# Output rows stored from two issuing queues, and another order for the last attention layer, in an interleaved S4 and sliding-attention kernel

## The chip, the cores and the metric

The kernel runs on one core of one Trainium2 chip. The time is the device time of one execution in microseconds (us), from the first to the last work of the program; each kernel is run several times and the median is given. The core's engines are TensorE (PE in the profile; PEld is its weight load), VectorE (DVE), ScalarE (ACT), GpSimd (POOL) and SyncE (SP, which here only issues DMA transfers). Each engine works through its own instructions strictly in the order in which the program gives them to it.

## The reference, cut to what matters

Four layers on a residual of 2048 positions by 512 channels in bfloat16: a state-space convolution (S4) and a sliding, dilated attention, twice.

```python
def _B_ref(x, wqkv, wo):                 # H = 32 heads of 16, W = 8, dil = 2
    qkv = (x @ wqkv).reshape(B, S, 3, H, Dh).transpose(2, 0, 3, 1, 4)
    q, k, v = qkv[0], qkv[1], qkv[2]
    idx = pos[:, None] - (jnp.arange(W) * dil)[None, :]
    mask = idx >= 0
    kg, vg = k[:, :, idx_c, :], v[:, :, idx_c, :]      # clipped at position 0
    logits = jnp.einsum("bhsd,bhswd->bhsw", q, kg) * scale
    attn = _softmax(jnp.where(mask[None, None], logits, -1e9), axis=-1)
    o = jnp.einsum("bhsw,bhswd->bhsd", attn, vg)
    return o.transpose(0, 2, 1, 3).reshape(B, S, D) @ wo

x = A_u
x = x + _A_ref(_layernorm(x), A_re, A_im, B_re, B_im, C_re, C_im, log_dt, Dskip)
x = x + _B_ref(_layernorm(x), wqkv, wo)
x = x + _A_ref(_layernorm(x), A_re, A_im, B_re, B_im, C_re, C_im, log_dt, Dskip)
x = x + _B_ref(_layernorm(x), wqkv, wo)
return x
```

## The kernel before

The residual stays on the chip in one tile X: 128 positions on the partitions, and on the free axis two halves of 256 channels, each with 16 row blocks (j = 0 to 15). The layers run one after the other: the convolution's kernel with the first convolution, `b_layer`, `a_layer`, `b_layer`. Only the last `b_layer` is touched by the change.

**How an order is made.** A layer does not emit instructions as it is written. It records operations in a `Plan`: `pl.op(engine, us, fn, *after)` is one step with the steps it comes after; `pl.either(name, way, way, ...)` records several ways of doing the same step. `Plan.run` then goes through a list of numbers, one string of `ORDERS` for each layer, and calls the functions in that order. A way whose numbers are not in the string does not exist in the program. So the string decides both the order on every engine and which engine does a step. The times and lags given to `pl.op` have no effect in the kernel.

**What the last layer does.**
- `start(q)`, for each quarter q of the positions (four row blocks) and each half cp of the channels: the block of X is turned so that channels lie on the partitions, either by a DMA transpose that SP issues (L1307) or by TensorE into the tile `pt_x` (L1301) and a copy (L1304). VectorE makes the layer norm's statistics (L1359) and joins them (L1363), ScalarE makes the roots (L1374).
- `pair` and `proj`: TensorE's q and k projections into `ps_qk` (L1439, L1420; four matmuls of 512 columns a group, or eight for a pair) and the copies to qT and kT (L1444, L1425), on ScalarE or VectorE. The keys of earlier positions are put beside the others by ScalarE, VectorE or a DMA (L1462).
- `pairs`: the norm's factors of neighbouring rows, moved down one partition by a small matmul (L1401), multiplied, spread by ScalarE to the tile RR (L1386), with POOL's ones for the first rows (L1392).
- `values`: v into VX (L1474, L1485, L1498).
- logits: VectorE's products of q and shifted k (L1519), a matmul that sums over a head's 16 channels into Lp (L1530), a copy to LT (L1548), a transpose into `pt_l` (L1556), a copy to L (L1561), and the multiplication by RR (L1599).
- softmax on VectorE (the sum's first step is L1580), with ScalarE and POOL.
- products with the values (L1695), summed by TensorE into `po`: either the flat way, 512 columns at a time (L1711), with a copy to `ot` (L1729) and a transpose back by TensorE (L1741) or by DMA (L1734); or the way of 128 columns (L1716) whose result needs no turn, with one copy (L1731).
- `out`: the output projection `ps_o` (L1795) and the residual's addition into X, in one of three ways: a VectorE addition (L1767); a ScalarE copy (L1773) and a VectorE addition (L1776); or a ScalarE copy and a DMA from POOL's queue that adds into X (L1779).
- `stored`: for each row block j a DMA of 128 rows by 512 channels to the output, after its addition, issued by SP (L1941).

Tiles are shared by rings: the products L1519 and L1695 have four buffers, `ps_qk` and most `ps_o` share two, `pt_x`, `po` and others two more.

Of the kernel before, what the change touches and what calls it, by code (L numbers as in the profile page):

```python
# [19 lines left out]
S = 2048  # L20
# [135 lines left out]
def halves(a):  # L156
    return a.rearrange("p (h c) -> p h c", h=2)
# [6 lines left out]
def turned_view(U):  # L164
    return U[:].rearrange("p j c -> p (j c)").rearrange("c (h j t p) -> c h j t p", h=2, j=NJ, t=2)
# [65 lines left out]
def load_params(nc, pp, prm):  # L231
# [75 lines left out]
]  # L307


# [1551 lines left out]
def kernel(  # L1861
# [16 lines left out]
    nc = tc.nc  # L1878
# [11 lines left out]
    X = kernel_and_first_conv(nc, tc, C, prm, A_u[0], const, kt_dram, eps, Wt)  # L1890
# [8 lines left out]
    ov = out[0].rearrange("(p j) d -> p j d", j=NJ)  # L1899
    with tc.tile_pool(name="mid", bufs=1) as mid:  # L1900
        U = mid.tile([128, NJ, D], BF, name="U")

        def summed(j, ps):
            if j // 4 not in BN_Q:
                nc.scalar.activation(X[:, :, j, :], halves(ps), ACT.Identity, accum_out=ln.sum[:, j:j + 1])
            else:
                nc.scalar.copy(X[:, :, j, :], halves(ps))

        def normed(pl, q, after):
            j0, j1 = q * 4, q * 4 + 4  # L1910

            def square(j):
                nc.scalar.activation(halves(U[:, j, :]), X[:, :, j, :], ACT.Square, bias=ln.nm[:, j:j + 1],
                                     accum_out=ln.sq[:, j:j + 1])

            def norm(j):
                nc.scalar.activation(halves(U[:, j, :]), X[:, :, j, :], ACT.Identity, bias=ln.nb[:, j:j + 1],
                                     scale=ln.rstd[:, j:j + 1])
            if q in BN_Q:
                for k in (j0, j0 + 2):  # L1920
                    o = [pl.op("V", 0.6, lambda j=j: ln.gather(X, 0, j, j + 1), after[j - j0]) for j in (k, k + 1)]
                    o = [pl.op("V", 0.09, lambda j=j: ln.gathered(j, j + 1), o[j - k]) for j in (k, k + 1)]
                    o = pl.op("A", 0.2, lambda k=k: ln.root(k, k + 2), *o)
                    o = pl.op("V", 0.08, lambda k=k: ln.offset(k, k + 2), o)
                    for j in (k, k + 1):
                        pl.mark(("u", j), pl.either(("norm2", j), lambda: pl.op("V", 0.32, lambda j=j: ln.norm(halves(U[:, j, :]), X[:, :, j, :], j), o),
                                                    lambda: pl.op("A", 0.71, lambda j=j: norm(j), o)))
                return
            o = pl.op("V", 0.12, lambda: nc.vector.tensor_scalar(ln.nm[:, j0:j1], ln.sum[:, j0:j1], -1.0 / D, None, ALU.mult),
                      *after)  # L1930
            o = [pl.op("A", 0.62, lambda j=j: square(j), o) for j in range(j0, j1)]
            o = pl.op("A", 0.2, lambda: ln.root_of_squares(j0, j1), *o)
            o = pl.op("V", 0.09, lambda: ln.offset_by(j0, j1), o)
            for j in range(j0, j1):
                a = pl.either(("norm2", j), lambda: pl.op("A", 0.71, lambda j=j: norm(j), o),
                              lambda: pl.op("V", 0.32, lambda j=j: ln.norm(halves(U[:, j, :]), X[:, :, j, :], j), o))
                pl.mark(("u", j), a)

        def stored(pl, q, after):
            for j, a in enumerate(after, q * 4):  # L1940
                pl.op("S", 0.45, lambda j=j: nc.sync.dma_start(ov[:, j, :].rearrange("p (h c) -> p h c", h=2), X[:, :, j, :]), a, lag=2.2)  # L1941
        b_layer(nc, tc, C, X, Wt, VX, turned_view(U), pst, eps, ln, True, summed, normed, BN_Q)
        a_layer(nc, tc, C, X, kt_dram, U)
        b_layer(nc, tc, C, X, Wt, VX, turned_view(U), pst, eps, ln, False, lambda j, ps: nc.scalar.copy(X[:, :, j, :], halves(ps)), stored, range(4))


# [28 lines left out]
```

## Time and profile before

| | us |
|---|---|
| Median of 3 runs | 431.56 (431.14 to 432.34) |
| Profiled execution, its own time | 430.11 |
| Span in the profile | 428.3 |
| Mean granted clock of TensorE | 0.999 of full speed |
| Last layer begins (first statistics) | 313.0 |
| Last addition into X ends | 423.8 |

All views are of one execution. Its own time is 1.8 us over the span, and 1.45 us under the median of the runs. In a timeline a row is a run of like instructions: start, duration, engine, line, operation, output tile <- input tile with shapes, the count after x, and in brackets the idle time ahead of it with what ended it. A DMA is seen twice: in the queue of the engine that issues it (SPq, ACTq), and as a transfer; "to landing" is from issue to the end of the transfer.

### The profile page before, as it was taken

To read this page: it belongs to the slowest core of one execution; us is meant where nothing else is said; L and a number is where in the kernel's file an instruction comes from. 1 tells how busy PE (TensorE), PEld (TensorE's weight loads), DVE (VectorE), ACT (ScalarE), POOL (GpSimd) and SP (SyncE) were. 2 spreads that over 40 slices of the span, in tenths; PEclk is the share of its full clock that TensorE was granted. 3 is DMA by queue.
4 is the path that set the end of the run, shared out by engine and by line. 5 is a ranking of instruction groups with operands and counts; after the bars stand their busy time and mean duration, and the time that the engine had idled before them with its cause. 6 is when DMAs were issued, how large, how long until landed. Compare 5 with 4: busy or idle time off the path is not lost.

```text
span 428.3 us, 11576 instructions
## 1 busy us (share of the span) xinstructions
PE 370.3 (86%) x4797; PEld 233.4 (54%) x4834; DVE 402.2 (94%) x682; ACT 320.9 (75%) x524; POOL 27.7 (6%) x97
## 2 busy tenths in 40 slices
PE   1277868897998889999997899899999999998995
PEld 1153646776887664347643345678864346643452
DVE  6999999999999789999899999999999899999994
ACT  6999999999998664668752578999957678752431
POOL 1000000000000200000000600020000000000240
PEclk9999999999999999999999999999999999999999
DMA  8996257597987774011223595199960000324295
GB/s 221 210 299 235 93 83 156 136 174 173 180 130 141 145 173 103 0 38 54 76 56 63 139 223 132 36 181 198 193 100 12 37 2 2 87 85 87 40 158 160
DMA packets 102203, 51.49 MB, mean 120 GB/s; under 512 B 81851, under 2 KB 94028, under 8 KB 101894
## 3 DMA queue, kind: packets, MB, share of 16 engines
q1 hardware_dynamic: 98758, 45.24, 49.1%
q0 software_dynamic: 3104, 5.24, 6.1%
q8 instruction: 38, 0.62, 0.7%
q10 hardware_dynamic: 288, 0.26, 0.2%
q14 instruction: 15, 0.12, 0.1%
HBM read 19.30 MB, written 6.29 MB: 60 GB/s over the span
## 4 chain that ended last, share of the span: by engine, by line
PE 48%; DVE 15%; ACT 14%; issue 4%; DMA 1%; ACTq 0%; DVEq 0%
PE po L1711 8%; PE ps_v L1474 7%; PE ps_qk L1420 7%; PE ps_qk L1439 6%; DVE prod L1695 5%; PE ps_o L1795 4%; PE Lp L1530 4%; PE psk L483 3%; DVE prod L1519 3%; ACT Z L875 2%; DVE pa L967 2%; PE ps_s L1117 2%; PE ps_s L872 1%; ACT sp_k L903 1%; PE vp L1183 1%
## 5 line engine op out<-in xcount | busy, mean ns | idle before, releaser
L1695 DVE TENSOR_TENSOR prod<-VX,L 128x512 bf16<-128x512 bf16 (+2 forms) x72 | 75.4, 1099 | 1.8 <-ACT VX L1485 1.0
L1519 DVE TENSOR_TENSOR prod<-qT,kT 128x4096 bf16<-128x4096 bf16 (+1 forms) x40 | 72.1, 1859 | 2.2 <-ACT kT L1462 1.0
L1711 PE MATMUL po<-prod,sb_ident 128*128 128x512 bf16 x233 | 56.4, 379 | 2.8 <-DVE prod L1695 2.0
L1711 PEld LDWEIGHTS <-sb_ident 128*128 128x128 bf16 x240 | 23.1, 97 | 31.3 <-issue 4.1
L875 ACT CAST Z<-ps_s 128x1024 bf16<-128x1024 f32 (+1 forms) x36 | 32.0, 932 | 0.5 <-PE ps_s L872 0.4
L1474 PE MATMUL ps_v<-wv,U 128*128 128x256 bf16 x256 | 31.4, 273 | 0.6 <-ACT VX L1485 0.3
L1795 PE MATMUL ps_o<-wo_t,oT 128*128 128x512 bf16 x124 | 31.4, 379 | 0.3 <-ACT oT L1744 0.2
L1729 ACT CAST ot<-po 128x1024 bf16<-128x1024 f32 (+1 forms) x16 | 15.1, 958 | 21.2 <-PE po L1711 21.2
L1420 PE MATMUL ps_qk<-U,wqk 128*128 128x512 bf16 x128 | 30.7, 380 | 0.3 <-ACT L L1658 0.3
L1485 ACT ACTIVATE VX<-ps_v,rs 128x256 bf16<-128x256 f32 x64 | 26.7, 473 | 5.6 <-PE ps_v L1474 5.1
L1439 PE MATMUL ps_qk<-U,wqk 128*128 128x512 bf16 x128 | 29.3, 379 | 0.0
L1474 PEld LDWEIGHTS <-U 128*128 128x128 bf16 x256 | 24.3, 97 | 8.9 <-issue 3.1
L1530 PE MATMUL Lp<-prod,sb_bones 128*32 128x512 bf16 x256 | 22.9, 383 | 3.0 <-DVE prod L1519 2.9
L1359 DVE BATCH_NORM_STATS2 pst<-X 128x6 f32<-128x256 bf16 x64 | 21.8, 407 | 0.5 <-ACT X L1209 0.5
L1420 PEld LDWEIGHTS <-wqk 128*128 128x128 bf16 x128 | 11.8, 98 | 16.8 <-issue 3.6
L1439 PEld LDWEIGHTS <-wqk 128*128 128x128 bf16 x128 | 12.2, 98 | 15.4 <-issue 1.6
L1795 PEld LDWEIGHTS <-oT 128*128 128x128 bf16 x128 | 12.2, 98 | 14.7 <-ACT oT L1744 0.7
L872 PE MATMUL ps_s<-KT,FK 128*128 128x128 bf16 (+1 forms) x360 | 18.8, 209 | 1.6 <-ACT KT L845 0.7
L967 DVE TENSOR_TENSOR pa<-sp_u,sp_k 128x2048 bf16<-128x2048 bf16 x16 | 19.3, 1220 | 0.8 <-ACT sp_k L903 0.5
L1171 DVE TENSOR_TENSOR pa<-xc,Kt 128x2048 bf16<-128x2048 bf16 x16 | 18.9, 1218 | 0.6 <-PE vp L1183 0.3
L892 PE MATMUL xp<-zt,sb_C 128*128 128x512 bf16 x45 | 15.0, 380 | 5.0 <-ACT zt L912 2.3
L872 PEld LDWEIGHTS <-FK 128*128 128x128 bf16 x360 | 17.4, 98 | 3.2 <-issue 2.3
(230 smaller groups left out, 841.1 us busy)
## 6 DMA issues: line engine op xcount, KB each, us to landing
kt_scratch<-sp_k SPq DMA_DIRECT2D x16, 256.0 KB, 3.0
Kt<-kt_scratch POOLq DMA_DIRECT2D x16, 256.0 KB, 6.6
sp_u<-sp_u SPq DMA_DIRECT2D x18, 128.0 KB, 2.7
X<-in_A_u_dram SPq DMA_DIRECT2D x8, 256.0 KB, 5.4
X<-in_A_u_dram SPq DMA_DIRECT2D x4, 512.0 KB, 5.6
Kt<-kt_scratch SPq DMA_DIRECT2D x8, 256.0 KB, 4.2
out_dram<-X SPq DMA_DIRECT2D x16, 128.0 KB, 2.0
VX<-VX SPq DMA_DIRECT2D x4, 448.0 KB, 3.7
```

The lines of the kernel that those rows point to most:

```text
L872: nc.tensor.matmul(ps[:, r, 0:n // 4, jj * 4:(jj + 1) * 4], w, x, start=(k == 0), stop=(k == len(todo) - 1))
L875: nc.scalar.copy(box["Z", kind, dc, b0][:, 0:n // 4, :, jq * 16:(jq + 1) * 16].rearrange("p g r k -> p r g k"), box.pop(("s1", kind, dc, j ...
L967: nc.vector.tensor_tensor(pr[:], box["U"][:, s:t + 1:t - s], k[:].unsqueeze(1).to_broadcast([128, 2, 1024]), ALU.mult)
L1420: nc.tensor.matmul(ps[:], wqk[:, ct, f0:f0 + 128], XT[:, ct // 2, 4 * s:4 * s + 4, ct % 2, :], start=(ct == 0), stop=(ct == 3))
L1439: nc.tensor.matmul(box[name][:, k * 512:k * 512 + 512], wqk[:, ct, f0:f0 + 128], XT[:, ct // 2, 4 * s:4 * s + 4, ct % 2, :], start=(ct == ...
L1474: nc.tensor.matmul(ps[:, jj].rearrange("p t h d -> p (t h d)"), XT[:, ct // 2, j + jj, ct % 2, :], wv[:, ct, fp * 256:(fp + 1) * 256], sta ...
L1485: nc.scalar.activation(out, ps, ACT.Identity, scale=r)
L1519: nc.vector.tensor_tensor(pr[:], windows(q, 0, 2), windows(kT[fp][:, a:a + n2, col(w):col(w) + 1024], -DIL * 128, 2), ALU.mult)
L1530: nc.tensor.matmul(Lp[r0:r0 + 32, w // 4, :], bones[:, w % 4 + k, :], pr[:, k, f2 - a, hb * 512:(hb + 1) * 512], start=(n == 1 and k == 0) ...
L1695: nc.vector.tensor_tensor(p2[:].rearrange("p w j t d h -> p w (j t) d h"), windows(v, -DIL * 256, taps), l.to_broadcast([128, taps, nj * 2 ...
L1711: nc.tensor.matmul(po[:, c:c + 512], ident[:], p2[:, t, k + j:k + j + 2].rearrange("p j t d h -> p (j t d h)"), start=first, stop=stop)
L1795: nc.tensor.matmul(ps, oT[:, ft // 2, o:o + 128], wo_t[:, ft, :], start=(ft == 0 and not res), stop=(ft == 3))
```

## The change

Two edits. `stored` gets a second way for each store: the queue of ScalarE instead of SP's. And the order string of the last layer is replaced. The orders of the other three layers are the same.

```diff
 ORDERS = [
 ...
-    "122 162 34 79 164 33 10 165 78 1 241 36 123 167 11 44 35 196 178 125 130 179 242 87 208 243 80 180 229 230 231 136 "
-    "325 40 181 50 182 183 326 81 77 197 198 119 120 38 93 209 244 82 210 215 126 245 246 121 259 268 76 269 270 232 233 "
...
-    "737 738 875 853 876 897 908 955 956 745 746 885 886 855 898 747 856 895 928 929 854 807 941 942 943 958 957 865 866 "
-    "896",
+    "34 120 87 44 164 1 76 178 130 122 78 162 77 79 36 94 95 163 136 81 208 168 253 254 255 119 121 199 35 7 209 210 50 "
+    "229 230 39 231 179 247 180 165 124 181 200 182 40 166 183 37 83 331 169 332 256 257 248 33 220 258 221 249 222 125 "
...
+    "873 874 808 709 705 703 868 869 707 710 924 968 893 894 909 940 941 953 954 955 969 883 884 907 814 904 906 972 974",
 ]
...
         def stored(pl, q, after):
             for j, a in enumerate(after, q * 4):
-                pl.op("S", 0.45, lambda j=j: nc.sync.dma_start(ov[:, j, :].rearrange("p (h c) -> p h c", h=2), X[:, :, j, :]), a, lag=2.2)
+                def store(queue, j=j):
+                    queue.dma_start(ov[:, j, :].rearrange("p (h c) -> p h c", h=2), X[:, :, j, :])
+                pl.either(("store", j), lambda: pl.op("S", 0.45, lambda store=store: store(nc.sync), a, lag=2.2),
+                          lambda: pl.op("A", 0.45, lambda store=store: store(nc.scalar), a, lag=2.3))
```

What the new string does, as the two programs stand against each other:
- The stores of row blocks 1, 6, 2, 11, 13 and 10 are issued by SP, in this order, those of 4, 5, 7, 0, 12, 3, 8, 9, 14 and 15 by ScalarE, in this order; store 12 waits for an adding DMA, and the five after it stand behind it.
- In `start` the half block turned by TensorE is the second half of quarter 2, copied by ScalarE; before it was the second half of quarter 0, copied by VectorE. That one, and the second half of quarter 1, come by DMA transposes.
- Of the joins and statistics of the norm, a part stands behind the first product L1519.
- One q copy of 1024 columns goes from ScalarE to VectorE; a k copy of 1024 becomes two of 512, and q copies of 512 are merged. Two key copies of L1462 go from ScalarE to DMAs of SP.
- The projections, their copies and RR's spread stand in another order towards each other; POOL's ones stand behind a mask of POOL.
- The fifteenth piece of the output goes the way of 128 columns (L1716, L1731) instead of the flat way with its turn back.
- Adding DMAs (L1779) are used for row blocks 4, 0, 1, 2, 3 and 12 (before 4, 3, 1, 0, 7, 6), the ScalarE copy with a VectorE addition for 6, 7 and 8 (before 5 and 12), the direct addition for the other seven (before eight).

22 rows, old and new, of the table ORDERS are left out of this document.

## The prediction

> **What bounds the kernel now.** I read the page first, for the span and the load of each engine.
>
> ```profile
> span 428.3 us, 11576 instructions
> PE 370.3 (86%) x4797; PEld 233.4 (54%) x4834; DVE 402.2 (94%) x682; ACT 320.9 (75%) x524; POOL 27.7 (6%) x97
> ```
>
> VectorE is busy 94% of the span and TensorE 86%, so a plan that only moves work can win what these two wait, and little more. The profiled execution took 430.11 us, the span 428.3 of it, 1.8 lie around it; the median of the runs is 431.56, so 1.45 us are added to a sum made against the profile. Everything ahead of the last attention layer is in the same order on every engine, so next I cut that layer into stages (us; then busy time and count of PE, PEld, DVE, ACT, POOL; granted clock; DMA share; GB/s).
>
> ```profile
> 313.00:327.50 14.50, 13.75 (x100) 7.68 (x99) 12.63 (x50) 8.40 (x13) 0.00 (x0) 1.00 0.39 55
> 327.50:339.30 11.80, 11.45 (x67) 4.48 (x66) 10.60 (x10) 6.81 (x19) 0.00 (x0) 1.00 0.09 34
> 339.30:402.20 62.90, 60.15 (x433) 31.48 (x434) 62.49 (x48) 39.43 (x77) 3.33 (x30) 1.00 0.19 47
> ...
> 411.10:424.00 12.90, 11.94 (x80) 6.05 (x78) 10.70 (x24) 4.05 (x7) 2.39 (x2) 1.00 0.79 158
> ...
> 424.00:426.00 2.00, 0.00 (x0) 0.00 (x0) 0.00 (x0) 0.00 (x0) 0.00 (x0) 1.00 0.88 245
> ```
>
> From 339.3 to 402.2 VectorE idles 0.41 us of 62.90: the middle moves with whatever moment it begins. The places to win are the start (VectorE waits 1.87 us to 327.5 and 1.20 us to 339.3), the end (2.2 us to 424) and the stretch after 424, where no engine computes and the DMA engines are at 0.88. The granted clock is 1.00 throughout, so it enters nowhere.
>
> **The start.** The timeline of VectorE, one row for a run of like instructions (start, us, what, count, wait ahead of it):
>
> ```profile
> 313.04 3.03 DVE L1359 BATCH_NORM_STATS2 pst<-X 128x6 f32<-128x256 bf16 x9
> ...
> 317.73 0.69 DVE L1304 COPY U<-pt_x 128x1024 bf16<-128x1024 bf16 x1 [0.45 <-issue]
> 318.34 5.31 DVE L1359 BATCH_NORM_STATS2 pst<-X 128x6 f32<-128x256 bf16 x16
> 323.57 0.41 DVE L1363 BATCH_NORM_AGGREGATE ln_mv_a<-pst 128x2 f32<-128x12 f32 x4
> ...
> 327.53 4.64 DVE L1519 TENSOR_TENSOR prod<-qT,kT 128x2048 bf16<-128x2048 bf16 x4 [1.00 <-ACT kT L1462]
> ...
> 337.98 1.23 DVE L1548 CAST LT<-Lp 128x1024 bf16<-128x1024 f32 x1 [0.70 <-PE Lp L1530]
> 339.32 8.89 DVE L1519 TENSOR_TENSOR prod<-qT,kT 128x4096 bf16<-128x4096 bf16 x4
> 348.12 0.68 DVE L1599 TENSOR_TENSOR L<-L,RR 128x1024 bf16<-128x1024 bf16 x1
> ...
> 402.19 0.42 DVE L1580 TENSOR_TENSOR sm<-L 128x512 bf16<-128x512 bf16 x1
> ```
>
> ScalarE's row gates the layer in both orders, and the chain of waits gives TensorE's steps and the key copy by DMA (start, us, what):
>
> ```profile
> 314.99 1.99 ACT L1209 CAST X<-ps_y 128x1024 bf16<-128x1024 f32 x3 [0.31 <-PE ps_y L1204]
> ```
>
> ```profile
> 317.03 0.61 PE pt_x L1301 x8
> 317.64 4.33 PE ps_qk L1439 x20
> ...
> 331.00 2.21 DMA kT<-kT
> ...
> 344.10 0.45 PE pt_l L1556 x8
> ...
> 348.34 0.97 PE ps_qk L1420 x4
> ```
>
> ```profile
> L1307 SPq DMA_TRANSPOSE U<-X x2: 1232/1282/1332, 317.0 to 318.3; - x2
> DMA to landing us min/median/max: 4.3/4.5/4.7
> ```
>
> The last X copy ends at 314.99 + 1.99 = 316.98. The new order turns another block on TensorE (third quarter, second half of the columns) and copies it on ScalarE, which takes 0.69 us from VectorE; the two transposes on SP go out about 1 us earlier, at 316.0 and 317.3, and land 4.3 to 4.7 later, by 322.0. VectorE: 11 statistics at 5.31/16 = 0.33 end at 316.7, it waits to 317.0, 19 more and 8 aggregates (0.41/4 each) end at 324.1. TensorE: two q/k matmuls and the turn end at 318.1, then 32 matmuls at 4.33/20 = 0.217 to 325.0, when the q pair is whole. So VectorE waits about 0.9 us and copies it itself, a copy moved here from ScalarE:
>
> ```profile
> L1444 DVE CAST qT<-ps_qk 128x1024 bf16<-128x1024 f32 x1 | 1.2, 1216 | 0.0
> ```
>
> With 1.14 net of overlap the first logit product starts at 326.2 instead of 327.5: 1.4 us gained. The two key copies of L1462 that ScalarE did are DMAs now; at 2.21 us, issued when ScalarE's k copies end, they land near 325, hidden under the q matmuls; without that cover they cost what they are late.
>
> Then eight products at 4.64/4 = 1.16, the 2 statistics and 8 aggregates that were moved behind the first of them (0.66 + 0.82) and the same 0.70 for the first Lp bring VectorE to the end of the LT copy near 338.6. ScalarE copies the last q quarter by about 338.85, because more q/k groups stand ahead of it on TensorE. The first 4096-wide product starts there, against 339.32: 0.47 of the 1.4 remains. Four of them at 8.89/4 end at 347.7. Next is L·RR (L1599), which needs POOL's ones in RR, behind ScalarE's spread:
>
> ```profile
> 344.62 1.08 ACT L1561 COPY L<-pt_l 128x512 bf16<-128x512 bf16 x2
> ```
>
> ```profile
> 340.52 1.14 ACT L1386 CAST RR<-rr 128x512 bf16<-128x512 f32 x2
> ```
>
> ```profile
> 341.25 0.87 POOL L1392 MEMSET RR<- 1x16 bf16 x10 [56.02 <-ACT RR L1386]
> ```
>
> In the new order TensorE reaches these transposes seven q/k groups after 338.2: 338.2 + 7 × 0.87 + 0.45 = 344.75; then the L copies 1.08, the spread 1.14, the ones 0.87, with 0.2 for the hops: 348.05. So L·RR starts there, against 348.12. **The start keeps 0.1 us**; the rest turns into this wait.
>
> **The middle.** The same instructions with VectorE 62.49 of 62.90 busy: the 0.1 is carried to 402.1, the softmax sum that was at 402.19. POOL's ones now stand behind a mask there; POOL is busy 3.33 us of 62.90. Bounds: 0.4 gained if all idle time goes; up to 1.2 lost if a wait such as that to 339.3 comes back. I take nothing.
>
> **The end.** One output piece, the fifteenth, goes without its turn back: 8 matmuls of 512 columns, a ScalarE copy, 4 transposes and another ScalarE copy are replaced by 32 matmuls of 128 columns and a VectorE copy.
>
> ```profile
> 256.46 2.08 PE L1716 MATMUL po<-sb_ident,prod 128*128 128x128 bf16 x28
> ```
>
> ```profile
> 423.13 0.69 DVE L1767 TENSOR_TENSOR X<-ps_o,X 128x512 bf16<-128x512 f32 x1 [0.17 <-PE ps_o L1795]
> ```
>
> TensorE loses 8 × 0.217 + 4 × 0.45/8 = 1.96 and gains 32 × 0.074 = 2.38 at the paced price, or 32 × 0.056 = 1.8 at the transposes': between 0.2 less and 0.4 more. As TensorE is 11.94 of 12.90 busy, that is nearly its whole effect; the round trip over ScalarE that goes was partly a stall. I take 0.2 gained, so the last X add ends near 423.5 instead of 423.82.
>
> **The stores.** Sixteen stores of 128 KB, all on SP before; the window's row is the last nine (ns shortest, median, longest; first and last issue).
>
> ```profile
> out_dram<-X SPq DMA_DIRECT2D x16, 128.0 KB, 2.0
> ```
>
> ```profile
> L1941 SPq DMA_DIRECT2D out_dram<-X x9: 435/443/1376, 420.2 to 425.4; - x9
> DMA to landing us min/median/max: 1.9/1.9/2.9
> ```
>
> ```profile
> L240 ACTq DMA_DIRECT2D raw_B_re<-in_A_B_re_dram x1: 450/450/450, 1.2 to 1.2; - x1
> ```
>
> ```profile
> L1779 POOL DMA_DIRECT2D X<-oT x6: 1178/1444/2138, 403.3 to 412.8; - x6
> DMA to landing us min/median/max: 3.3/4.6/5.7
> ```
>
> ```profile
> 416.69 0.58 ACT L1773 CAST oT<-ps_o 128x512 bf16<-128x512 f32 x1 [1.83 <-PE ps_o L1795]
> ```
>
> SP issues the last store at 425.4, 1.6 us after the last add: SP has a queue of its own making. The last landing is 425.4 + 1.9 = 427.3. Ten stores on ScalarE's queue, at 450 ns against 443, cost ScalarE 4.5 us, beside 4.05 busy of 12.90: it has room, though copies queued behind a waiting store (that of row block 0 behind store 4) start late. The rate of 245 GB/s at 0.88 of the DMA engines is one store in 0.535 us; at full share one in 0.47. The accumulating additions in POOL's queue change their rows, with one at row block 12 late: its ScalarE copy ends about 417, as the row at 416.69 shows for a neighbour, and its data land 3.3 to 5.7 later, say at 421.2. Store 12 waits for it on ScalarE, with five stores queued behind it, and three of SP's are still to go. Nine stores then take 9 × 0.47 to 0.535, and the last needs 1.9 − 0.5 = 1.4 over its own slot: 421.2 + 1.4 + 4.2 to 4.8 = 426.8 to 427.4. Against 427.3, 0.2 gained. **The sum**: 430.11 − 0.1 (start) − 0 (middle) − 0.2 (end and stores; the earlier last add lies inside the same transfers) = 429.8, or 431.2 with the 1.45 us to the median, rounded down. A measurement of this kernel can tell about 0.3%, 1.3 us, from no change, so this counts as the same.
>
> **Rivals.** B, two queues drain the tail freely: the last store goes out right behind the last add at 423.5 and lands at 425.4, 1.9 us earlier; 431.56 − 1.9 − 0.1 = 429.6. For it: issue at 443 ns per store is close to the 535 ns pitch, and SP alone issues. Against it: a share of 0.88 leaves 12%, and eight stores of 0.535 can then win about 0.5 us. The Trainium skill, "DMA: Bandwidth & Descriptors", section "Issuing engines are not separate DMA queues", speaks against this change: DMAs that any engine starts run on the same 16 DMA engines, and several issuers save only the sequencer's time. By that rule the tail wins at most the half microsecond, and the sum is 431.0; by the issue times alone it wins 1.6 and the sum is 429.9. The row of 0.88 stands with the rule.
>
> C, slower: the chain to L·RR at 348 becomes the bound. If the seven groups take 0.97 each, as at 348.34, that is 0.7 more, and if two more copies of 0.58 stand ahead of the L copies on ScalarE, 1.16 more: the ones end at 349.9, VectorE stands 1.8 us longer than before, and the full middle carries it to the end: 431.56 + 1.8 − 0.2 = 433.2. It decides once the ones end after 348.12 + 1.3 = 349.4. For it: TensorE has nearly no slack there (60.15 of 62.90). Against it: most groups run at 0.87.
>
> D, also slower, at the end: the addition of row block 12 lands at its slowest, 5.7 us after 417.1, at 422.8; ScalarE's queue stands and nine stores end at 422.8 + 1.4 + 4.8 = 429.0, 1.7 us later: 433.2. It decides from a landing at 422.3.
>
> E, nothing moves, since each gain meets the next wait: 431.5; it shares the forecast's side.
>
> **How the numbers follow.** Forecast with E 0.41, B with or without more of the start 0.31, C 0.18, D 0.10. The predicted time is the forecast's, 431.2. The range goes down to B with the 0.4 us of the start that L·RR swallowed and 0.3 us for the runs' spread, 428.9, and up to C and D with 0.2 us, 433.4. Faster by over 0.3% is B, 0.31; the same 0.41; slower 0.28.
>
> **What would show it.** First product at L1519 near 326.2, first 4096-wide one near 338.9; a wait ahead of L1599 put down to POOL or to the L copy, with its start near 348.0 (C: near 350); the sum at L1580 near 402.1; last add near 423.5; stores at a mean above 240 GB/s to a last landing near 427. The forecast is wrong if the first L1599 starts over 1.3 us away from 348.1, if stores 3, 8, 9, 14 and 15 go out ahead of 420 (B) or all behind 422.3 (D), or if the middle shows a new wait of a microsecond or more on VectorE.

## The result and the profile after

The changed kernel takes 433.81 us (median of 12 runs, 432.60 to 435.51) against 431.01 us (12 runs of before): a ratio of 1.0064, 95% interval 1.0045 to 1.0082. It is slower by 2.8 us, outside the stated range of 428.9 to 433.4. The profiled execution took 432.86 us, 2.75 over that of before, and its span is 2.8 us longer, so the two traces show the loss whole. In the changed kernel every line number below the replaced string is one lower (L1579 is L1580 before); the stores are L1941 in both.

The page of the changed kernel begins so:

```profile
span 431.1 us, 11649 instructions
```

VectorE's timeline of the changed kernel (start, us, what, count, wait ahead of it), at the places that the prediction named:

```profile
326.56 3.50 DVE L1518 TENSOR_TENSOR prod<-qT,kT 128x2048 bf16<-128x2048 bf16 x3
...
339.26 8.90 DVE L1518 TENSOR_TENSOR prod<-qT,kT 128x4096 bf16<-128x4096 bf16 x4 [0.36 <-ACT qT L1443]
348.08 0.69 DVE L1598 TENSOR_TENSOR L<-L,RR 128x1024 bf16<-128x1024 bf16 x1
...
350.73 8.91 DVE L1518 TENSOR_TENSOR prod<-qT,kT 128x4096 bf16<-128x4096 bf16 x4 [0.19 <-ACT qT L1424]
...
402.62 0.42 DVE L1775 TENSOR_TENSOR X<-oT,X 128x512 bf16<-128x512 bf16 x1
402.96 0.42 DVE L1579 TENSOR_TENSOR sm<-L 128x512 bf16<-128x512 bf16 x1
...
420.89 0.69 DVE L1766 TENSOR_TENSOR X<-ps_o,X 128x512 bf16<-128x512 f32 x1 [1.78 <-PE ps_o L1794]
...
424.94 0.69 DVE L1766 TENSOR_TENSOR X<-ps_o,X 128x512 bf16<-128x512 f32 x1 [0.17 <-PE ps_o L1794]
```

ScalarE's last X copy, which gates the layer, is the first mark to compare:

```profile
315.21 1.99 ACT L1208 CAST X<-ps_y 128x1024 bf16<-128x1024 f32 x3 [0.31 <-PE ps_y L1203]
```

It ends at 317.20, 0.22 later than before (316.98), although nothing ahead of it was changed: that much the layers ahead differ between two executions. The last softmax sum begins at 402.96 against 402.19, +0.77: 0.22 of it came in with the layer, 0.34 is an addition into X (L1775) that the new order has ahead of the sum, 0.21 was lost on the way. From the sum to the end of the span it is 431.1 − 402.96 = 28.14 us, before 428.3 − 402.19 = 26.11. **So 2.03 of the 2.80 us are lost in the tail behind the last softmax sum.** I use this tail to compare the experiments: their profiled executions reach the sum anywhere from 402.6 to 405.4. That difference comes in ahead of the last layer: up to ScalarE's last X copy the mean granted clock is 0.95 to 1.00, and the copy ends anywhere from 316.9 to 320.2, though the layers ahead are the same in all. From there to the last addition the clock is 1.00 in all eleven traces, and from the copy's end to the sum it is 85.21 to 85.22 us in the four traces of the old order and 85.75 to 85.76 in the seven of the new one.

The chain of waits of the changed kernel, its last part (it ends with the last addition; the stores behind that are not in it):

```profile
412.12 1.01 ACT ot L1728
...
413.16 6.18 DMA oT<-ot
...
419.39 1.47 PE ps_o L1794 x6
...
424.94 0.69 DVE X L1766
```

A DMA stands in it for 6.18 us: the third transpose of the output. Here is that line (L1733, in the stretch of 411 to 417; the third is the slower of the two), and the same line of before (L1734):

```profile
L1733 SPq DMA_TRANSPOSE oT<-ot x2: 1233/1498/1762, 411.4 to 413.2; - x2
...
DMA to landing us min/median/max: 4.4/5.3/6.2
```

```profile
L1734 SPq DMA_TRANSPOSE oT<-ot x1: 1302/1302/1302, 413.1 to 413.1; - x1
...
DMA to landing us min/median/max: 4.2/4.2/4.2
```

What else ran in the DMA engines shows in POOL's timeline, which issues the adding DMAs; first the changed kernel's, then before's:

```profile
410.77 2.38 POOL L1778 DMA_DIRECT2D X<-oT  x2 [6.25 <-ACT oT L1772]
413.92 2.38 POOL L1778 DMA_DIRECT2D X<-oT  x2 [0.77 <-ACT oT L1772]
418.25 1.17 POOL L1778 DMA_DIRECT2D X<-oT  x1 [1.94 <-ACT oT L1772]
```

```profile
406.00 3.59 POOL L1779 DMA_DIRECT2D X<-oT  x3 [1.42 <-ACT oT L1773]
412.09 2.39 POOL L1779 DMA_DIRECT2D X<-oT  x2 [2.50 <-ACT oT L1773]
```

POOL issues in order. In the new order the add of row block 0 stands ahead of those of 1 and 2, and its data come late (ScalarE's copy at 409.88), so POOL idles 6.25 us while the copies of 1 and 2 are done by 407. Where three adds went out from 406 to 409.6 and two from 412.1 before, four go out now from 410.8 to 416.3, and one at 418.25. The stretches of one microsecond of the changed kernel show the DMA engines empty and then full (the last two columns are DMA share and GB/s):

```profile
410.00:411.00 1.00, 1.00 (x6) 0.39 (x4) 0.83 (x3) 1.00 (x2) 0.23 (x1) 1.00 0.00 0
...
415.00:416.00 1.00, 1.00 (x10) 0.47 (x8) 1.00 (x4) 0.58 (x1) 1.00 (x2) 1.00 1.29 185
...
424.00:425.00 1.00, 0.91 (x5) 0.20 (x2) 0.75 (x2) 0.00 (x0) 0.00 (x0) 1.00 0.02 5
...
426.00:427.00 1.00, 0.00 (x0) 0.00 (x0) 0.00 (x0) 0.00 (x0) 0.00 (x0) 1.00 1.00 272
```

The second empty stretch, at 424, is the other place. Row block 12's add goes out at 418.25 and lands after 5.9 us; ScalarE's queue shows who waited for it:

```profile
417.44 0.38 ACTq L1941 DMA_DIRECT2D out_dram<-X  x1
424.15 3.64 ACTq L1941 DMA_DIRECT2D out_dram<-X  x6
```

Store 12 is issued at 424.15 and five stores behind it, of data that are mostly older. SP's queue stood in the same stretch (us in total, times, longest wait):

```profile
SPq L1941 <- DMA out_dram<-X: 3.6, 2, 2.8
```

Its store of row block 11, whose addition is the first of a run of three from 422.65 and ended by about 423.4, went out at 424.38, when an earlier store of SP had landed; its last one waited for a store of ScalarE to land. Why a store should wait for another the runs do not show, but the empty stretch is not store 12's alone. My theory T: the loss comes from the transfers' new order, in two places: late adds that delay the third transpose (and with it TensorE and the last addition), and store 12's wait, behind which the stores pile up. Rivals: R1, stores from two queues disturb the rest; R2, the new order of projections at the start costs it.

### The profile page after: what moved, and what is told of

Read it like the earlier page. It is cut to its first block, busy times and chain, and to the rows that moved or that the text cites. A ratio compares the mean times of both kernels' runs of the same rounds, so it can differ in the third digit from the quotient of the medians.

```text
span 431.1 us, 11649 instructions
## 1 busy us (share of the span) xinstructions
PE 373.8 (87%) x4854; PEld 233.8 (54%) x4854; DVE 403.3 (94%) x683; ACT 319.1 (74%) x521; POOL 27.6 (6%) x97
## 5 line engine op out<-in xcount | busy, mean ns | idle before, releaser
L1710 PE MATMUL po<-prod,sb_ident 128*128 128x512 bf16 x232 | 54.9, 379 | 3.0 <-DVE prod L1694 2.9
L1710 PEld LDWEIGHTS <-sb_ident 128*128 128x128 bf16 x232 | 22.2, 98 | 31.1 <-issue 4.2
L1794 PE MATMUL ps_o<-wo_t,oT 128*128 128x512 bf16 x128 | 32.5, 379 | 1.0 <-DMA oT<-ot 0.8
L891 PE MATMUL xp<-zt,sb_C 128*128 128x512 bf16 x64 | 18.9, 379 | 4.0 <-ACT zt L911 2.3
L1794 PEld LDWEIGHTS <-oT 128*128 128x128 bf16 x128 | 11.9, 98 | 15.3 <-DMA oT<-ot 1.3
```

What stands on the lines that cost most here:

```text
L1710: nc.tensor.matmul(po[:, c:c + 512], ident[:], p2[:, t, k + j:k + j + 2].rearrange("p j t d h -> p (j t d h)"), start=first, stop=stop)
L1794: nc.tensor.matmul(ps, oT[:, ft // 2, o:o + 128], wo_t[:, ft, :], start=(ft == 0 and not res), stop=(ft == 3))
```

## The experiments

Tails are in us from the last softmax sum; before 26.11 with the last addition's end at 21.63, the changed kernel 28.14 and 22.67. Ratios are to runs of before taken beside each version, with the 95% interval; the medians of different experiments are not to be compared directly.

**Old order, two queues** (`old_two_queues`).

```diff
-nc.sync.dma_start(ov[:, j, :]...
+(nc.scalar if j in (7, 8, 9, 15) else nc.sync).dma_start(ov[:, j, :]...
```

> The order of before, with the stores of row blocks 7, 8, 9 and 15 issued by ScalarE's queue in place of SP's. Theory T (the new order of the last layer's transfers costs the time, the split of the stores by itself does not): last addition near 423.8 as before, the backlog of SP at the end gone, DMA at 270 to 300 GB/s after 424 instead of 245, last landing near 426.2 instead of 427.0: 0.5 to 1.0 us faster than before. Rival R1 (two issuing queues disturb each other and the other transfers): 1 us or more slower than before. Rival R2 (the new order of projections at the start of the layer costs it): no statement here, as T.

Measured: 0.9984 (0.9967 to 1.0001), tail 428.6 − 403.22 = 25.38 us. Its marks in VectorE's timeline, the span, and the DMA share at the end:

```profile
403.22 0.42 DVE L1580 TENSOR_TENSOR sm<-L 128x512 bf16<-128x512 bf16 x1
...
424.17 0.69 DVE L1767 TENSOR_TENSOR X<-ps_o,X 128x512 bf16<-128x512 f32 x1 [0.17 <-PE ps_o L1795]
```

```profile
core 0: 428.6 us, clock 0.996
```

```profile
424.00:426.00 2.00, 0.13 (x1) 0.00 (x0) 0.69 (x1) 0.00 (x0) 0.00 (x0) 1.00 1.02 283
```

The last addition keeps its place in the tail (21.64) and the DMA engines run at 283 GB/s instead of 245. Splitting the stores is by itself a gain of 0.73 us in the tail; the ratio's interval just reaches 1. R1 falls.

**New order, all stores on SP** (`new_all_sync`).

```diff
-lambda: pl.op("A", 0.45, lambda store=store: store(nc.scalar), a, lag=2.3)
+lambda: pl.op("A", 0.45, lambda store=store: store(nc.sync), a, lag=2.3)
```

> The changed kernel with all sixteen stores on SP, in the same order of the list. T: the adding DMAs and the transpose are as late as in the changed kernel, and store 12 now blocks SP, with eight stores behind it at 0.53 us: 0.3 to 1.0 us slower than the changed kernel, 3 to 4 us slower than before. R1: back to within 1 us of before. R2: the same as the changed kernel, 2.8 us slower than before.

Measured: 1.0067 (1.0051 to 1.0083), 433.31 us, tail 431.2 − 403.47 = 27.73. As slow as the changed kernel, not slower as T had it: SP is blocked by store 12 now, but row block 12's add landed after 5.1 us instead of 5.9, so that store 12 went out 20.4 us after the sum instead of 21.2, and the third transpose landed after 5.7 us instead of 6.2. R1 falls a second time: without any second queue the loss stays.

**Store 12 last** (`new_store12_last`). The number of store 12 goes to the end of the string.

```diff
-... 924 968 893 ... 906 972 974",
+... 924 893 ... 906 972 974 968",
```

> The changed kernel with store 12 put at the end of the list, so that ScalarE's stores 3, 8, 9, 14 and 15 no longer stand behind its wait. T: the last addition stays at 425.6, the stores fill the idle stretch of 423 to 425, last landing near 427.7 instead of 429.3: 1.3 to 1.7 us faster than the changed kernel, 1.1 to 1.5 slower than before. R1 and R2: within 0.5 us of the changed kernel.

Measured: 1.0045 (1.0030 to 1.0060), 432.54 us.

```profile
403.57 0.42 DVE L1579 TENSOR_TENSOR sm<-L 128x512 bf16<-128x512 bf16 x1
...
426.28 0.69 DVE L1766 TENSOR_TENSOR X<-ps_o,X 128x512 bf16<-128x512 f32 x1 [0.17 <-PE ps_o L1794]
```

```profile
core 0: 430.7 us, clock 0.996
```

The tail is 27.13, 1.01 shorter, though in this execution the transpose took 6.9 us and the last addition ended 23.40 after the sum, 0.73 later than in the changed kernel. The end came earlier while the computation ended later: it hung on store 12 and on what stood behind it. T had hoped for 1.3 to 1.7, from a last landing at 429.3 in the changed kernel; there the last store, issued at 427.04, landed at 430.1. Up to the third transpose the two programs are the same, so by 0.7 us its landing differs between executions by itself.

**Adds of 1 and 2 early** (`new_adds_early`). The adds of row blocks 1 and 2 (786, 796) are put right behind that of row block 4 (824), ahead of row block 0's (776).

```diff
-... 583 824 856 775 581 776 ...
+... 583 824 786 796 856 775 581 776 ...
```

> The changed kernel with the adding DMAs of row blocks 1 and 2 put ahead of that of row block 0 in POOL's queue. T: they go out near 407 to 409, in the stretch of 409 to 412 in which the DMA engines were idle, the third transpose of the output lands within 4.5 us of its issue instead of 6.2, TensorE's wait of 0.8 for it goes, last addition near 424.8, and the adding DMA of row block 12 lands in 4 to 5 us: 0.8 to 1.6 us faster than the changed kernel. R1: the transpose stays as late, within 0.3 us of the changed kernel. R2: within 0.3 us too.

Measured: 1.0035 (1.0018 to 1.0051), 431.85 us. The transposes in the stretch from 411 to 417, two marks, and the span:

```profile
L1733 SPq DMA_TRANSPOSE oT<-ot x2: 1232/1481/1730, 413.6 to 415.3; - x2
...
DMA to landing us min/median/max: 4.1/4.3/4.6
```

```profile
405.13 0.42 DVE L1579 TENSOR_TENSOR sm<-L 128x512 bf16<-128x512 bf16 x1
...
426.17 0.69 DVE L1766 TENSOR_TENSOR X<-ps_o,X 128x512 bf16<-128x512 f32 x1 [0.17 <-PE ps_o L1794]
```

```profile
core 0: 431.6 us, clock 0.966
```

The transpose lands within 4.6 us, the last addition ends 21.73 after the sum, as before's does within 0.1, and the tail is 26.47, 1.67 shorter: the last addition is 0.94 earlier, and store 12 went out 19.31 after the sum instead of 21.19, 1.88 earlier.

**Both** (`new_both`).

> Both edits to the changed kernel: the adding DMAs of row blocks 1 and 2 early in POOL's queue, and store 12 last. T: the two gains are of different places, so they add: from the last softmax sum (first row of L1579 after 402) to the end 25.3 to 25.8 us, where before took 26.1, the changed kernel 28.1, adds early alone 26.5 and store 12 last alone 27.1; 0 to 0.5 us faster than before. If the two only share one cause: 26.3 or more, no better than the adds alone.

Measured: 0.9993 (0.9977 to 1.0009), 430.93 us.

```profile
402.62 0.41 DVE L1579 TENSOR_TENSOR sm<-L 128x512 bf16<-128x512 bf16 x1
```

```profile
core 0: 428.1 us, clock 0.999
```

The tail is 25.48. Two savings of 1.01 and 1.67 from 28.14 would make 25.46: they add. Three moved numbers in a list of some 400 take back the whole loss, with the new start, the new middle and the ten stores on ScalarE as they are. R2 keeps the 0.55 us that the new order takes longer from the X copy to the sum, 0.34 of it the addition that stands there. So the new order, mended like this, is level with before, and its tail is no shorter than the 25.38 of the old order with two queues: the trace shows no gain beyond that of the split stores.

**Old order, adds late** (`old_adds_late`), the same from the other side. The adds of row blocks 3, 1 and 0 (806, 786, 776) and store 3 (810) go behind the add of row block 7 (850).

> The order of before with the adding DMAs of row blocks 3, 1 and 0 (and store 3) put behind that of row block 7 in POOL's queue, so that five of them go out from 412 on. T, from the other side: the third transpose, issued near 413, lands after 5.5 us or more instead of 4.4, TensorE waits for it at the output projection of row block 10, the last addition is 0.8 to 1.5 us later and the span from the last softmax sum to the end 27 to 28 us against 26.1. If the delay of the transpose in the changed kernel had another cause: within 0.3 us of before.

Measured: 1.0048 (1.0031 to 1.0066), 434.04 us. It is as slow as expected, and not for the reason expected:

```profile
405.37 0.42 DVE L1580 TENSOR_TENSOR sm<-L 128x512 bf16<-128x512 bf16 x1
...
426.31 0.69 DVE L1767 TENSOR_TENSOR X<-ps_o,X 128x512 bf16<-128x512 f32 x1 [0.17 <-PE ps_o L1795]
```

```profile
core 0: 433.2 us, clock 0.965
```

```profile
416.23 1.30 SPq L1734 DMA_TRANSPOSE oT<-ot  x1
420.91 9.79 SPq L1941 DMA_DIRECT2D out_dram<-X  x15
```

The last addition ends 21.63 after the sum, exactly as before, and the transpose landed within 4.2 us. But a store of SP waits for a late add until 420.91, fifteen stores go out in one queue from there, and the tail is 27.83. So late adds with a queue of stores behind them cost 1.7 us without any late transpose. And of the five late adds none delayed it: POOL had begun to issue two of them, at 415.28 and 416.00, and finished neither when SP began the transpose at 416.23; three came behind it. In the changed kernel two were issued to the end in the 2.4 us ahead of it (410.77 to 413.16). The next run tests that.

**One add ahead of the transpose** (`new_one_add_ahead`). The add of row block 1 and its store (786, 809) go behind the add of row block 3 (806).

> The changed kernel with the adding DMA of row block 1, and SP's store 1 behind it, put after that of row block 3: of the two adding DMAs that go out in the 2.4 us ahead of the third transpose one is left, the other follows the transpose. T, as corrected by the order of before with late adds (adds that follow the transpose did not delay it): the transpose lands 4.1 to 4.7 us after its issue instead of 6.2, TensorE's wait for it goes, the last addition comes 21.6 to 21.9 us after the last softmax sum instead of 22.7. But row block 12's add is no earlier, so the end stays at 27.7 to 28.3 us after that sum (28.1), the median within 0.4 us of the changed kernel's: what sets the end is store 12's wait. Rival (TensorE's wait sets the end): the end 0.8 to 1.0 us earlier too. Rival (any five adds within 8 us delay the transpose): the transpose lands after 5.5 us or more as in the changed kernel.

Measured: 1.0034 (1.0015 to 1.0052), 432.47 us.

```profile
L1733 SPq DMA_TRANSPOSE oT<-ot x2: 1232/1492/1753, 412.0 to 413.7; - x2
...
DMA to landing us min/median/max: 4.2/4.3/4.5
```

```profile
403.49 0.42 DVE L1579 TENSOR_TENSOR sm<-L 128x512 bf16<-128x512 bf16 x1
...
424.52 0.69 DVE L1766 TENSOR_TENSOR X<-ps_o,X 128x512 bf16<-128x512 f32 x1 [0.17 <-PE ps_o L1794]
```

```profile
core 0: 430.6 us, clock 0.972
```

The transpose is back at 4.5 us or less and the last addition at 21.72, as T had it. The tail is 27.11, 1.03 shorter, which T had not: the add of row block 12 landed earlier too, store 12 went out 1.0 us earlier after the sum, and the end with it. This run alone doesn't tell the two causes, the late transpose and store 12's wait, apart.

**TensorE's wait filled** (`new_hole_filled`). The last matmuls of the fifteenth piece (709, 705, 703, 707) go ahead of the projections of row blocks 8 and 9.

> The changed kernel with TensorE's last 16 matmuls of the fifteenth output piece put ahead of the projections of row blocks 8 and 9, which wait for the late transpose. T: the wait of 0.8 us is filled and the last addition comes 0.5 to 0.8 us earlier, but the end is set by store 12's wait and the nine stores behind it (issued from 424.15 on, whatever TensorE does), so the time moves by less than 0.3 us. Rival (TensorE's wait alone sets the end): 0.5 to 0.8 us faster than the changed kernel.

Measured: 1.0051 (1.0032 to 1.0069), 433.62 us. My edit made a new wait: VectorE's copy of the piece now stands behind the addition of row block 9, which comes later, and the last projections wait for that copy, so the last addition ended 23.78 after the sum, 1.1 later than in the changed kernel instead of earlier.

```profile
403.17 0.42 DVE L1579 TENSOR_TENSOR sm<-L 128x512 bf16<-128x512 bf16 x1
...
426.26 0.69 DVE L1766 TENSOR_TENSOR X<-ps_o,X 128x512 bf16<-128x512 f32 x1 [0.17 <-PE ps_o L1794]
```

```profile
core 0: 431.5 us, clock 1.000
```

The tail is 28.33 all the same, 0.19 longer. With store 12 last the computation ended 0.73 later and the end came 1.01 earlier; here it ended 1.11 later and the end hardly moved. In the changed kernel the end follows store 12, not the last addition.

**Old order, two queues, two stores early** (`old_two_early`), the version to which the runs point: stores 7, 0, 15 and 9 on ScalarE's queue, 7 and 0 right behind ScalarE's last copy.

> The order of before, with the stores of row blocks 7, 0, 15 and 9 on ScalarE's queue and those of 7 and 0, whose additions have landed by then, moved ahead of the last five additions, right behind ScalarE's last copy. T: between 419.8 and 422 the DMA engines are at 0.15 to 0.57, so these two cost nothing there, two stores fewer are left at the end: last landing 1.0 to 1.5 us earlier than before, the span from the last softmax sum to the end 24.6 to 25.1 (stores on two queues without the move: 25.4). If the rate of the DMA engines at the end doesn't matter: 25.4.

Measured: 0.9977 (0.9960 to 0.9995), 430.23 us.

```profile
404.75 0.42 DVE L1580 TENSOR_TENSOR sm<-L 128x512 bf16<-128x512 bf16 x1
```

```profile
core 0: 429.6 us, clock 0.964
```

The tail is 24.85, 1.26 shorter than before's, as expected. It is the only version here whose interval lies below 1. That interval overlaps with the one of the old order with two queues, so the 0.53 us that the two early stores add rest on one trace of each.

## Why the prediction was wrong, point by point

**The start: right.** With the 0.22 taken off, the first product began at 326.34 (forecast 326.2), the first 4096-wide one at 339.04 (338.85), the first L·RR at 347.86 (348.05, before 348.12). So 0.26 was kept there, against 0.1. One step was wrong in kind: no wait for POOL's ones showed ahead of L1598. They ended at 347.75, and VectorE came through its own products only at 348.08, after a wait of 0.36 us for a q copy. That the forecast of L·RR fits to 0.2 us is in part luck. A slip went unnoticed too: the terms listed up to the end of the LT copy add up to 338.9, not 338.6. Rival C did not occur.

**The middle: within its bounds.** The sum came 0.21 late where 0.1 gained was forecast. With the 0.26 kept at L·RR, some 0.5 went back in the middle, 0.19 of it the wait for a q copy at 350.73; the range of 0.4 gained to 1.2 lost held it, the value of nothing did not.

**The end: the step that failed.** I priced the fifteenth piece at 0.2 less to 0.4 more, and that holds: with the transpose in time the last addition ends 21.72 or 21.73 after the sum, 0.1 after before's 21.63. What I left out is the landing of the third transpose, which I took for granted, and POOL's queue: I listed which row blocks are added by DMA and did not walk the order in which POOL issues them. The new order puts row block 0's late add ahead of two ready ones. That cost 0.94 at the last addition (22.67 to 21.73 in the run with adds early), where the sum had 0.2 gained; in the run with store 12 last, where the transpose landed later still, it was 1.67. The end of the program followed the stores, though, and these the same queue.

**The stores: the term that was mis-sized.** Row block 12's data I let land at 421.2, issued at 417.1, which is 4.1 us, 15.0 after the forecast sum. They were issued at 418.25, 15.3 after the measured sum, and landed 5.9 us later, beyond the 5.7 of the row that I had as the upper end. With the adds of 1 and 2 early the same add was issued 15.3 after the sum too and landed after 4.0: so POOL's order made it slow. The DMA engines' share was 1.18 to 1.35 in each microsecond from 418 to 422; that the adds share them with one another, the transpose and the stores is the likely way, and not shown. Store 12 went out at 424.15, not at 421.2: of the 2.95 us some 0.9 came with the later sum, 0.3 with the issue, 1.8 with the landing. The rest of the working holds: nine stores and the pace of 0.47 to 0.535 us each (272 GB/s in the stretch of 426 to 427 is 0.48), after an empty stretch at 424. From 424.15 it gives 429.8 to 430.4 for the last landing, and that was at 430.1. Moving the store away from the queue's head gave 1.01 back, POOL's order alone 1.67, both together 2.66 of a tail that had lost 2.03; the surplus is about what the split of the stores gains in the old order.

**The rivals.** D is what happened, at the place that it named: the landing was at 424.1, past the point from which it decides (422.3). It had 0.10, and its price was computed for a landing at 422.8, so the range ended too early as well. One condition was there to be worked out: the copies that POOL waits for and the order of its queue follow from the list. B's mechanism exists, and its size was between the two bounds: old order, two queues gained 0.73 in the tail where the free share of 0.88 gave 0.5 and the issue times 1.6. The Trainium skill's rule ("DMA: Bandwidth & Descriptors", "Issuing engines are not separate DMA queues") points to the right one of the two: the share rises from 0.88 to 1.02, and the gain is nearer to the 0.5 than to the 1.6. E did not occur.

## What to carry to other kernels

When a change touches which DMAs an engine issues, walk every issuing queue in order, GpSimd's too: find the first entry that isn't ready, and count what stands ready behind it. A store that waits for a late transfer belongs at the end of its queue, whatever engine that is; here this cost 1.0 us, and a late add put ahead of two ready ones cost 1.7, while the split of the stores for which the order was redone was worth 0.7. Compare tails from a mark close ahead of the change: the layers ahead, shared by all, moved by some 3 us between executions.

## What the runs showed that I had not expected

The delay of a DMA transpose depended on what had been issued shortly ahead of it, not on how full the engines were meanwhile. With two adding DMAs that POOL had issued to the end in the 2.4 us ahead of it, the third transpose landed after 5.7 to 6.9 us (6.2, 5.7, 6.9 and 6.5 in the changed kernel, with all stores on SP, with store 12 last and with the filled wait). With one such add (adds early, both, one add ahead), or with two that POOL had begun and was still issuing (before, and the other runs of the old order), it landed after 4.1 to 4.2, even where three more adds followed it at once. In the 4 us from its issue the DMA engines' share was 1.22 in the changed kernel, where it took 6.2 us, and 1.19 with adds early, where it took 4.1. The four late runs also have in common that the second add was issued between two transposes 1.7 us apart; the runs do not tell these two descriptions apart. Why the order of issue decides so sharply they do not show either.
